# Gated linear attention followed by an MoE layer: two neighbouring tokens on one partition

## The chip, the cores and the metric

The kernel runs on one core of one Trainium2 chip. The metric is the device time of the core in microseconds (us), read from repeated executions. A span on a profile page is some 1.8 us shorter than the device time of the same execution, because the page counts from the first to the last instruction. PE is TensorE, DVE is VectorE, ACT is ScalarE, POOL is GpSimd, SP is SyncE (here it only issues DMAs).

## The reference

```python
# q, k, v, alpha: [B=4, H=8, S=768, D=48] float32, alpha in 0.8 .. 1.0
for t in range(S):                       # gated linear attention
    state = alpha[:, :, t, :, None] * state + k[:, :, t] (outer) v[:, :, t]
    y[:, :, t] = q[:, :, t] @ state
x = y.transpose(0, 2, 1, 3).reshape(3072, 384)
h = x @ w_in                             # 384 -> 2048
r = np.maximum(h, 0)
g = s * (r * r) + b
out = g @ w_out                          # 2048 -> 384, float32
```

The kernel cuts the sequence into 24 chunks of 128 tokens. Inside a chunk the running product of alpha, `b`, is the exponential of a running sum of logarithms. q is multiplied by `b` and k by `1/b`; then the causal part of a chunk is an ordinary masked matrix product, and one state per chunk carries the rest.

## The kernel before

A partition is a token of the chunk, so a load of one tensor and chunk moves 128 x 8 rows of 48 floats: packets of 192 bytes.

```python
def load(n, src, dst):                    # 4 tensors x 24 chunks, issued from SP
    nc.sync.dma_start(
        out=dst[n % NIN],                 # [128, H, D] fp32
        in_=src[b, :, c * C : (c + 1) * C, :].rearrange("h s d -> s h d"))

def st_ln(n):     # ACT: la = ln(alpha)
def st_cum(n):    # PE:  running sum, U_bf (upper triangular) @ la, and its last row
def st_exp_b(n):  # ACT: b_s  = exp(cum)
def st_exp_i(n):  # ACT: binv = exp(-cum), blast = exp(last row)
def st_vcast(n):  # POOL: vb = bf16(v)

def st_qb(n):     # DVE, both inputs in SBUF
    nc.vector.tensor_tensor(out=qk_sb[n % 3][:, 0, :, 0:D],
                            in0=q_in[n % NIN], in1=b_sb[n % 2], op=ALU.mult)
def st_kb(n):     # DVE, the same with k and binv
# ... st_T + st_Tcopy (PE, DVE) for the first 12 chunks, a DMA transpose from SP after that
# ... st_KV, st_t1, st_snew: the state (PE, DVE, POOL)
# ... st_A (PE), st_mask (DVE), st_y (PE), st_yevac (ACT), then a transpose of y

def relu(w):      # ACT: r = max(h, 0), bf16, 128x512          96 times
def square(w):    # DVE: gt = r * r, both inputs in SBUF       96 times
# mm1 (w_in) and mm2 (w_out) on PE are the bulk of PE's work
```

Nothing is ordered by hand. Each step is declared with an engine, an assumed duration in us and a priority. A list scheduler in the kernel then fixes one order for every engine before the program is built. The engines run those orders strictly, each its own.

```python
op("SP", 0.45, ranks[x, n], load, n, src, dst, w=[(x, n % NIN)], lat=1.2, dma=1.03)
op("ACT", 0.43, t - 1.0, st_ln, n, r=[("a", ii)], w=[("la", i2)])
op("DVE", 0.52, t + 0.2, st_qb, n, r=[("q", ii), ("b", i2)], w=[("qb", i3)])
op("SP", 0.5, -3000, st_Tdma, n, r=[("qb", i3), ("kb", i3)], w=[("qkT", i3)], lat=TLAT, dma=1.6)
op("DVE", 0.36, t + 1.0, square, w, r=[("r", w % 2)], ...)
op("SP", 0.5, -2000, ostore, x, r=[os], dma=0.55)
```

Loads, DMA transposes and stores all sit in SP's one order.

## Time and profile before

The median over 4 executions is 194.23 us (193.64 to 194.85).

| | before |
|---|---|
| median time | 194.23 us |
| PE / DVE / POOL busy | 173.8 / 133.0 / 54.7 us |
| time of all DMA packets on 16 engines | 155.4 us, of which 96.3 are the 192-byte input packets (15.7 ns each) |
| last w_out quarter in SBUF | 39.7 us |

First, lines of the profile page: the span, the busy times, and three of the rows that cut the span into 40 slices (a digit is the busy share in tenths; PEclk is the granted clock of PE).

```profile
span 192.8 us, 4631 instructions
...
PE 173.8 (90%) x1769; PEld 112.7 (58%) x1780; DVE 133.0 (69%) x232; ACT 114.0 (59%) x251; POOL 54.7 (28%) x90
...
DVE  4474636999979999999786735987565883354321
...
POOL 6332413406533465242434352313231100000000
PEclk9996999999999999999999999999999999999999
```

DVE stands at 9 in twelve slices, eleven of them between 33 and 92 us. Next, the busy time of each engine in four stretches (columns: stretch, length, PE, PE weight loads, DVE, ACT, POOL, granted clock, DMA share, GB/s).

```profile
0.00:40.00 40.00, 27.78 (x396) 21.75 (x397) 24.00 (x41) 19.39 (x40) 14.18 (x32) 0.96 0.98 212
40.00:90.00 50.00, 48.29 (x622) 36.66 (x621) 47.89 (x81) 39.58 (x96) 21.12 (x29) 1.00 0.99 202
90.00:150.00 60.00, 58.71 (x518) 33.15 (x525) 41.86 (x73) 38.87 (x88) 18.68 (x28) 1.00 0.97 194
150.00:192.00 42.00, 38.99 (x239) 21.10 (x239) 19.21 (x40) 16.13 (x29) 0.69 (x1) 1.00 0.20 61
```

So the DMA engines are close to full until 150 us (share 0.97 to 0.99), DVE is nearly full from 40 to 90 us, and PE is full after 90 us. The chain of waits (start, length, what) shows the DMA side of it; these are its longest DMA pieces:

```profile
29.75 9.89 DMA wst<-in_moe_w_out_dram
...
52.62 8.65 DMA a_in<-in_alpha_dram x2
...
98.82 4.58 DMA a_in<-in_alpha_dram
...
132.76 2.98 DMA a_in<-in_alpha_dram
```

Last, the groups of DVE instructions whose two inputs both lie in SBUF (busy us, mean ns of one, then the idle time ahead of them).

```profile
L579 DVE TENSOR_TENSOR gt<-r 128x512 bf16<-128x512 bf16 x96 | 43.9, 474 | 14.6 <-ACT r L567 13.8
...
L389 DVE TENSOR_TENSOR qk<-q_in,b_s 128x384 bf16<-128x384 f32 x24 | 16.0, 666 | 10.7 <-ACT b_s L379 6.1
L397 DVE TENSOR_TENSOR qk<-k_in,binv 128x384 bf16<-128x384 f32 x24 | 15.3, 641 | 6.3 <-DMA k_in<-in_k_dram 5.8
```

These means hide two populations. In the trace a q or k product lasts 554 or 552 ns on average when POOL is idle and 760 or 705 ns when it overlaps a POOL instruction; a square lasts 420 or 564 ns. (The count takes any POOL instruction but DMA issues, short semaphore instructions included; without those, a few of the 144 change sides.)

### The profile page before, as it was taken

What the parts mean: (1) busy time and instruction counts of PE and PEld (TensorE: products, weight loads), DVE (VectorE), ACT (ScalarE), POOL (GpSimd) and SP (SyncE); (2) the same over time, 40 slices, a digit from 0 to 9 for tenths busy, and PEclk for the clock granted to TensorE, in tenths of its full rate; (3) what the DMA queues carried; (4) which work ended last, traced back from release to release, by engine and by line L of the source; (5) the groups of instructions that cost most, each with busy time, mean ns of one, the idle gap of its engine ahead of it and who ended that gap; (6) DMA issues with size and microseconds to landing.
All of it is one profiled execution on the core that took longest, in us unless ns stands there. A gap on an engine that the chain in (4) does not pass through costs nothing.

```text
span 192.8 us, 4631 instructions
## 1 busy us (share of the span) xinstructions
PE 173.8 (90%) x1769; PEld 112.7 (58%) x1780; DVE 133.0 (69%) x232; ACT 114.0 (59%) x251; POOL 54.7 (28%) x90
## 2 busy tenths in 40 slices
PE   3857777899997999999999999999899999999992
PEld 3635666477685786775554564646564556445650
DVE  4474636999979999999786735987565883354321
ACT  2425525999675877797786756578346661576000
POOL 6332413406533465242434352313231100000000
PEclk9996999999999999999999999999999999999999
DMA  5999999989899999999999999997999612200212
GB/s 101 192 174 188 160 225 383 312 168 208 184 233 196 223 182 221 187 208 185 196 206 180 185 181 191 226 190 155 203 224 178 132 22 65 82 32 9 73 56 82
DMA packets 124151, 32.76 MB, mean 170 GB/s; under 512 B 117472, under 2 KB 124128, under 8 KB 124128
## 3 DMA queue, kind: packets, MB, share of 16 engines
q1 hardware_dynamic: 122240, 30.88, 74.5%
q0 software_dynamic: 1600, 1.57, 5.3%
q8 instruction: 14, 0.23, 0.5%
q14 instruction: 9, 0.07, 0.1%
q10 hardware_dynamic: 288, 0.00, 0.1%
HBM read 25.17 MB, written 4.72 MB: 155 GB/s over the span
## 4 chain that ended last, share of the span: by engine, by line
PE 53%; SPq 15%; DMA 14%; DVE 8%; ACT 5%; issue 4%; POOL 0%; DVEq 0%; ACTq 0%
PE bank L586 23%; PE bank L558 22%; SPq L294 12%; DMA a_in<-in_alpha_dram 8%; DMA wst<-in_moe_w_out_dram 5%; SPq L310 2%; PE a_ps L473 2%; DVE gt L579 2%; ACT r L567 1%; DVE am L482 1%; PE bank L506 1%; PE bank L365 1%; DVE qk L397 1%; DVE qkT L416 1%; DVE qk L389 1%
## 5 line engine op out<-in xcount | busy, mean ns | idle before, releaser
L567 ACT ACTIVATE r<-bank 128x512 bf16<-128x512 f32 x96 | 56.2, 607 | 35.0 <-PE bank L558 20.7
L558 PE MATMUL bank<-xd,w_in_bf 128*128 128x128 bf16 (+2 forms) x469 | 71.8, 295 | 5.3 <-DMA w_in_bf<-in_moe_w_in_dram 4.7
L586 PE MATMUL bank<-w_out_bf,gt 128*128 128x384 bf16 x384 | 70.4, 326 | 0.6 <-ACT w_out_bf L318 0.4
L579 DVE TENSOR_TENSOR gt<-r 128x512 bf16<-128x512 bf16 x96 | 43.9, 474 | 14.6 <-ACT r L567 13.8
L558 PEld LDWEIGHTS <-w_in_bf 128*128 128x128 bf16 x480 | 37.9, 99 | 25.5 <-DMA w_in_bf<-in_moe_w_in_dram 5.3
L586 PEld LDWEIGHTS <-gt 128*128 128x128 bf16 x384 | 35.6, 97 | 23.8 <-issue 1.3
L482 DVE TENSOR_TENSOR am<-a_ps,mask 128x1024 bf16<-128x1024 f32 x24 | 29.3, 1219 | 3.0 <-PE a_ps L473 2.6
L386 POOL CAST vb<-v_in 128x384 bf16<-128x384 f32 x24 | 14.6, 611 | 52.1 <-DMA v_in<-in_v_dram 43.2
L462 POOL TENSOR_TENSOR s_st<-t,blast 64x192 bf16<-64x192 bf16 x32 | 20.0, 626 | 26.3 <-DVE t L455 15.6
L358 ACT ACTIVATE la<-a_in 128x384 bf16<-128x384 f32 x24 | 12.7, 529 | 18.5 <-DMA a_in<-in_alpha_dram 17.9
L389 DVE TENSOR_TENSOR qk<-q_in,b_s 128x384 bf16<-128x384 f32 x24 | 16.0, 666 | 10.7 <-ACT b_s L379 6.1
L397 DVE TENSOR_TENSOR qk<-k_in,binv 128x384 bf16<-128x384 f32 x24 | 15.3, 641 | 6.3 <-DMA k_in<-in_k_dram 5.8
L595 DVE SCALAR_TENSOR_TENSOR o_sb<-bank,s_col,bias_w 128x384 f32<-128x384 f32 x12 | 7.4, 617 | 14.3 <-PE bank L586 14.2
L618 POOL TENSOR_TENSOR o_sb<-o_sb,bias_w 128x384 f32<-128x384 f32 x12 | 12.6, 1057 | 8.2 <-ACT o_sb L609 6.8
L379 ACT ACTIVATE b_s<-bank 128x384 f32<-128x384 f32 x24 | 11.9, 496 | 4.1 <-PE bank L370 3.6
L519 ACT ACTIVATE yn<-bank 128x384 bf16<-128x384 f32 x24 | 11.9, 495 | 2.5 <-PE bank L506 2.5
L382 ACT ACTIVATE binv<-bank 128x384 f32<-128x384 f32 x24 | 12.1, 503 | 0.1
L455 DVE TENSOR_TENSOR t<-bank,s_st 128x384 bf16<-128x384 f32 x16 | 8.8, 551 | 4.0 <-PE bank L432 2.7
L473 PE MATMUL a_ps<-qkT 64*128 64x128 bf16 x192 | 9.8, 223 | 0.9 <-DVE qkT L416 0.7
L416 DVE COPY qkT<-bank 128x1024 bf16<-128x1024 bf16 x12 | 8.2, 682 | 2.6 <-PE bank L409 2.6
L740 PE MATMUL bank<-zeros_bf 128*64 128x64 bf16 x112 | 6.8, 225 | 3.4 <-DVE zeros_bf L263 3.1
L365 PE MATMUL bank<-la,U_bf 128*128 128x384 bf16 x24 | 8.2, 340 | 1.5 <-ACT la L358 1.5
(47 smaller groups left out, 135.6 us busy)
## 6 DMA issues: line engine op xcount, KB each, us to landing
k_in<-in_k_dram SPq DMA_DIRECT2D x24, 192.0 KB, 4.2
a_in<-in_alpha_dram SPq DMA_DIRECT2D x24, 192.0 KB, 3.9
q_in<-in_q_dram SPq DMA_DIRECT2D x24, 192.0 KB, 4.0
v_in<-in_v_dram SPq DMA_DIRECT2D x24, 192.0 KB, 3.8
out_dram<-o_sb SPq DMA_DIRECT2D x24, 192.0 KB, 2.5
wst<-in_moe_w_out_dram SPq DMA_DIRECT2D x4, 768.0 KB, 11.2
w_in_bf<-in_moe_w_in_dram POOLq DMA_DIRECT2D x4, 384.0 KB, 6.8
qkT<-qk SPq DMA_TRANSPOSE x12, 4.0
```

The lines of the kernel that those rows point to most:

```text
L294: nc.sync.dma_start(out=dst[n % NIN], in_=src[b, :, c * C : (c + 1) * C, :].rearrange("h s d -> s h d"),)
L358: nc.scalar.activation(out=la_sb[n % 2][:, :, 0:D], in_=a_in[n % NIN], func=AF.Ln)
L386: nc.gpsimd.tensor_copy(out=vb_sb[n % 3], in_=v_in[n % NIN])
L389: nc.vector.tensor_tensor(out=qk_sb[n % 3][:, 0, :, 0:D], in0=q_in[n % NIN], in1=b_sb[n % 2], op=ALU.mult,)
L397: nc.vector.tensor_tensor(out=qk_sb[n % 3][:, 1, :, 0:D], in0=k_in[n % NIN], in1=binv_sb[n % 2], op=ALU.mult,)
L462: nc.gpsimd.tensor_tensor(out=s_sb[n % 2][rows, :, cols], in0=t1_sb[n % 2][rows, :, cols], in1=blast_sb[n % 2][rows].unsqueeze(2).to_broad ...
L473: nc.tensor.matmul(out=a_ps[:, e, p, :], lhsT=qkT[64 * e : 64 * e + 64, 1, p, :], rhs=qkT[64 * e : 64 * e + 64, 0, p, :], start=True, stop ...
L482: nc.vector.tensor_tensor(out=am_sb[n % 2].rearrange("a e p t -> a (e p) t"), in0=a_ps.rearrange("a e p t -> a (e p) t"), in1=mask.unsquee ...
L558: nc.tensor.matmul(out=hp[:, i * n : (i + 1) * n], lhsT=w_in_bf[:, kk, 128 * j : 128 * (j + 1)], rhs=xd_sb[g % 3][:, kk, 0:n], start=(kk = ...
L567: nc.scalar.activation(out=r_sb[w % 2], in_=bank("h", w), func=AF.Relu)
L579: nc.vector.tensor_tensor(out=dst, in0=r, in1=r, op=ALU.mult)
L586: nc.tensor.matmul(out=op[:, 0:d_model], lhsT=gt_sb[:, slot, j, :], rhs=w_out_bf[:, j, :], start=(j == 0), stop=(j == NJ - 1),)
```

## The change

The intent is larger packets and less work per token. A partition now holds two neighbouring tokens, so a packet is 2 x 48 floats, 384 bytes, and one load serves a pair of chunks. ln and the exponentials are taken once per pair of tokens; the token's own share of the decay is put back by products with alpha:

```diff
+    def load(m, src, dst):                 # pair m, 12 pairs
+            out=dst[m % NIN].rearrange("i h t d -> i h (t d)"),
+            in_=src[b, :, c * C : (c + 2) * C, :].rearrange("h (i t) d -> i h (t d)", t=2),

+    def st_ap(m, eng):                     # ap = alpha0 * alpha1
+        eng.tensor_tensor(out=ap_sb[m % 2], in0=a[:, :, 0], in1=a[:, :, 1], op=ALU.mult)
+    def st_pre(m, x, eng):                 # q0 *= alpha0, q1 *= ap, k0 *= alpha1
+        t, s, w = ((qt, 0, a[:, :, 0]), (qt, 1, ap_sb[m % 2]), (kt, 0, a[:, :, 1]))[x]
+        eng.tensor_tensor(out=t[:, :, s], in0=t[:, :, s], in1=w, op=ALU.mult)
+    # ap on POOL from pair 3 on, st_pre on POOL from pair 2 on (30 instructions)

+    def st_vcross(m):                      # v copied across the partition halves
+        eng.dma_start(out=vt_sb[m % 2][hi, 0], in_=vb_sb[m % 2][lo, 1])
+        eng.dma_start(out=vt_sb[m % 2][lo, 1], in_=vb_sb[m % 2][hi, 0])

+    def st_Tdma(m):                        # DMA transposes of 64 rows, two per pair
+        for c in range(2):
+            nc.sync.dma_start_transpose(
+                in_=qk_sb[m % 2][R * c : R * c + R].rearrange("a x u e d -> a (x u e d)"), ...)

     def ostore(x):                         # 48 stores of 64 rows instead of 24 of 128
+        for t in range(2):
+            nc.sync.dma_start(out=..., in_=out_sb[(x // 4) % NOUT][R * t : R * t + R])

-GROUPS = [1, 1, 2, 1, 1, 2, 4, 4, 4, 4]
+GROUPS = [2, 2, 2, 2, 4, 4, 4, 4]
-UNIT = 1.62
+UNIT = 1.4
-NIN = 9                                    # buffers of input chunks
+NIN = 4                                    # buffers of input pairs
-N_POOL_BIAS = 12
+N_POOL_BIAS = 4
# ... 8 common PSUM banks instead of 6 and a fixed pair, 64-row matmuls for the state,
# ... new durations and priorities for the list scheduler, which orders everything anew
```

## The prediction

> **What bounds the kernel now** (busy times in stretches, timeline, chain of waits).
>
> - 0 to 40 us, loading: DMA share 0.98. The first MoE matmul runs at 16.5 us, matmuls wait for w_in until 30.3, the last w_out arrives at 39.7.
> - 40 to 150 us: DMA share still 0.97 to 0.99; DVE 47.9 of 50 us until 90. The chain holds three long DMA waits for alpha (8.7, 4.6, 3.0 us).
> - 150 us to the end: DMA share 0.20, PE alone.
>
> PE is 90% busy on the page, but the Trainium skill ("Perfetto Trace Analysis", Identifying the Most-Contended Engine) warns that pipelined matmul busy time misleads. From start to start a 128x384 matmul costs 162 ns, not the page's 326; all useful matmuls sum to about 155 us. About 16 us of it is done by 40 us (24 lost), about 98 of 110 in the middle (12 lost); the tail is full.
>
> **What the change does.**
>
> DMA: 98304 input packets of 192 B become 49152 of 384 B. The packet records give 15.7 ns for 192 B and 65 to 75 ns for 1536 B; a line between them gives my estimate of 22 to 23 ns at 384 B. On 16 engines 96 us becomes 70: minus 26. The skill ("DMA: Bandwidth & Descriptors", Specifications) puts line rate at 512 B and more; 384 B stays below, so time does not halve. Given back: more DMA transposes (14 chunks instead of 12 for q/k, 12 instead of 10 for y; +4 us) and v copies across halves (+3). Total about 155 to 135 us.
>
> ACT: ln and exps once per pair: 12 x (0.53+0.50+0.50+0.20) = -21 us; 114 to about 92; not the limit.
>
> POOL: alpha product, pre-multiplies, v cast and v keep: 55 to about 90 us.
>
> DVE: +5 us (alpha product and pre-multiplies of the first pairs), +5 (8 more output evictions of 0.62), -2 (transposed copies). POOL contention, from overlaps in the trace: q/k products last 554 ns alone and 705 to 760 beside POOL, squares 420 against 564; more POOL work adds about 4 us. DVE: 133 to about 145 us.
>
> PE: same columns; 155 us stays.
>
> **Critical path.** Start: two pairs (8 x 1.45), w_in (10.2) and w_out (about 9) must arrive: last w_out near 34 us instead of 39.7. First MoE matmul stays near 17 us: a pair holds twice the data and has a longer chain. Gain 5 us. Middle: the waits for alpha disappear and some 7 of 12 lost us come back; the rest stays, since DVE needs about 6.3 us per chunk against PE's 6.45 until chunk 10. Tail unchanged. Of 26 us less DMA time only about 12 reach the span.
>
> **Prediction:** 182.5 us, 8 in 10 between 175 and 190. Faster by over 2%: 0.83; within 2%: 0.13; slower: 0.04.
>
> **What would show each step.** Input packets at 22 to 23 ns; last w_out at 33 to 36 us; waits for alpha in the middle gone from the chain, PE matmul lines over 60% of it; DVE over 140 us, and 95% busy between 40 and 90 us; qk and gt means above 670 and 475 ns; POOL 80 to 100 us.
>
> **What would make it wrong.** 384 B packets at 30 ns (no DMA gain): 190 or more. POOL pre-multiplies slower than 1 us each, with the alpha product on POOL ahead of ln: chunks come late, PE starves. DVE saturating: 187 or more. Longer latency per pair with only two buffers for q/k. On the good side, if DVE keeps up, PE's 155 us plus 15 us start and 4 us tail allows 174.

## The result, and the profile after

The median is 210.91 us over 4 executions (209.48 to 211.76). The ratio is 1.085, with a 95% interval of 1.078 to 1.092: slower by 8.5%. Ratios are the mean time of one kernel's fast runs over that of the other's fast runs of the same rounds on the same chip, so they are not quite the ratio of the medians that stand beside them.

| | before | predicted | after |
|---|---|---|---|
| median time, us | 194.23 | 182.5 | 210.91 |
| last w_out quarter in SBUF, us | 39.7 | 33 to 36 | 32.9 |
| input packets, ns each | 15.7 | 22 to 23 | 23.3 |
| all input packets on 16 engines, us | 96.3 | 70 | 71.7 |
| all packets on 16 engines, us | 155.4 | 135 | 154.9 |
| DVE busy, us | 133.0 | 145 | 165.5 |
| POOL busy, us | 54.7 | 90 | 100.7 |
| mean granted clock of PE | 0.990 | (not said) | 0.955 |

The same lines of the page:

```profile
span 209.1 us, 4551 instructions
...
PE 182.5 (87%) x1693; PEld 114.6 (55%) x1693; DVE 165.5 (79%) x271; ACT 99.3 (47%) x196; POOL 100.7 (48%) x142
...
DVE  4796698999999999999999999999967444444321
...
POOL 7661412694959999967695644656520000000000
PEclk9995799995899997999999999999999999999998
```

DVE stands at 9 in 24 slices instead of twelve, POOL is nearly full from 63 to 89 us, and the clock row has dips that before did not have. The stretches:

```profile
0.00:40.00 40.00, 31.23 (x377) 24.50 (x378) 31.11 (x57) 21.56 (x39) 18.34 (x46) 0.91 1.03 266
40.00:90.00 50.00, 41.48 (x442) 28.77 (x440) 49.31 (x68) 24.16 (x54) 43.34 (x49) 0.90 0.78 180
90.00:150.00 60.00, 55.30 (x533) 31.46 (x532) 58.83 (x94) 32.50 (x70) 36.95 (x45) 1.00 0.91 187
150.00:192.00 42.00, 41.58 (x271) 22.45 (x270) 22.26 (x48) 19.97 (x35) 2.10 (x4) 1.00 0.36 64
```

From 40 to 150 us DVE is busy 108.1 of 110 us. The others wait for it (ACT is idle for 29.8 us ahead of its relus until a square is done), while the DMA share falls to 0.78 between 40 and 90 us: the DMA engines are no longer the limit there. The same three groups, and one of the new POOL groups:

```profile
L652 DVE TENSOR_TENSOR gt<-r 128x512 bf16<-128x512 bf16 x96 | 56.8, 612 | 16.3 <-ACT r L640 15.8
...
L464 DVE TENSOR_TENSOR qk<-k_in,binv 128x384 bf16<-128x384 f32 x24 | 21.9, 942 | 0.1
L456 DVE TENSOR_TENSOR qk<-q_in,b_s 128x384 bf16<-128x384 f32 x24 | 20.0, 858 | 0.0
...
L402 POOL TENSOR_TENSOR k_in<-k_in,a_in 128x384 f32<-128x384 f32 x10 | 11.4, 1139 | 2.7 <-DMA k_in<-in_k_dram 2.5
```

The three DVE groups have the same counts and the same shapes as before, yet they take 98.7 us instead of 75.2: 23.5 us more for identical instructions. Ahead of the products DVE is idle for only 0.1 and 0.0 us in all, so it hardly ever waits for their inputs. Here the two engines stand side by side for a few microseconds (timeline of after: start, length, engine, line, operation):

```profile
70.01 2.40 DVE L456 TENSOR_TENSOR qk<-q_in,b_s 128x384 bf16<-128x384 f32 x2
70.68 1.31 POOL L695 TENSOR_TENSOR o_sb<-o_sb,bias_w 128x384 f32<-128x384 f32 x1
...
75.19 2.04 DVE L464 TENSOR_TENSOR qk<-k_in,binv 128x384 bf16<-128x384 f32 x2
...
75.50 1.31 POOL L402 TENSOR_TENSOR q_in<-q_in,a_in 128x384 f32<-128x384 f32 x1
```

Two products that would last about 1.1 us alone take 2.0 to 2.4 us while POOL works on SBUF tensors (an output bias, which before has too, in the first pair of lines; a new product in the second). Split as before, a q or k product lasts 548 or 550 ns alone and 939 or 1073 ns overlapping POOL; a square 419 or 782 ns. Alone they have not changed at all. And DVE's instructions with only one input in SBUF (the other in PSUM) do not lengthen: in after a mask of 128x512 lasts 679 ns beside POOL (31 of them) and 679 ns alone (17).

The chain of waits of after can only be followed back to 113 us; two of its pieces that have no like in before, and its longest wait for a DMA:

```profile
120.52 1.63 DVE qk L456 x2
122.15 1.76 DVE qk L464 x2
...
144.00 3.76 DMA k_in<-in_k_dram
```

One more view is needed, since PE's busy time misleads: on the page a 128x384 matmul lasts some 330 ns, but at full clock the next one starts 162 ns after it. From the trace I counted the useful PE work done by a given time: each matmul at that distance to the next one, or less where the next started sooner. This is an estimate worked out from the trace, good to about 2 us, since some records are missing and short matmuls are hard to price.

| useful PE work (us) done by | 40 us | 90 us | 100 us | 150 us |
|---|---|---|---|---|
| before | 15 | 60 | 68 | 113 |
| after | 18 | 50 | 57 | 100 |

After is 2 to 3 us ahead at 40 us, as meant. It is 11 us behind at 100 us and 13 behind at 150 us. The loss is made from 40 to 100 us, where DVE is full.

### The profile page after: what moved, and what is told of

It reads as the page before. It is cut to its first block, busy times and chain, and to the rows that moved or that the text cites. A ratio compares the mean times of both kernels' runs of the same rounds, so it can differ in the third digit from the quotient of the medians.

```text
span 209.1 us, 4551 instructions
## 1 busy us (share of the span) xinstructions
PE 182.5 (87%) x1693; PEld 114.6 (55%) x1693; DVE 165.5 (79%) x271; ACT 99.3 (47%) x196; POOL 100.7 (48%) x142
## 5 line engine op out<-in xcount | busy, mean ns | idle before, releaser
L640 ACT ACTIVATE r<-bank 128x512 bf16<-128x512 f32 x96 | 57.0, 599 | 56.6 <-DVE gt L652 29.8
L631 PE MATMUL bank<-xd,w_in_bf 128*128 128x256 bf16 (+1 forms) x384 | 76.8, 334 | 2.4 <-DVE gt L652 1.0
L652 DVE TENSOR_TENSOR gt<-r 128x512 bf16<-128x512 bf16 x96 | 56.8, 612 | 16.3 <-ACT r L640 15.8
L556 DVE TENSOR_TENSOR am<-bank,mask 128x512 bf16<-128x512 f32 x48 | 30.0, 679 | 1.1 <-PE bank L547 1.1
L464 DVE TENSOR_TENSOR qk<-k_in,binv 128x384 bf16<-128x384 f32 x24 | 21.9, 942 | 0.1
L402 POOL TENSOR_TENSOR q_in<-q_in,a_in 128x384 f32<-128x384 f32 x10 | 12.0, 1205 | 15.3 <-DMA q_in<-in_q_dram 15.1
L591 ACT ACTIVATE yn<-bank 128x384 bf16<-128x384 f32 x24 | 11.5, 488 | 14.4 <-PE bank L578 14.4
L447 POOL COPY vt<-vb 64x384 bf16<-64x384 bf16 x24 | 14.2, 591 | 6.2 <-ACT vb L440 4.9
L474 PE MATMUL bank<-ident_bf,qk 128*128 128x128 bf16 x80 | 9.0, 264 | 4.5 <-DVE qk L456 2.6
L402 POOL TENSOR_TENSOR k_in<-k_in,a_in 128x384 f32<-128x384 f32 x10 | 11.4, 1139 | 2.7 <-DMA k_in<-in_k_dram 2.5
L578 PE MATMUL bank<-vt,am 128*128 128x48 bf16 x192 | 9.7, 185 | 3.1 <-DMA vt<-vb 1.3
L402 POOL TENSOR_TENSOR q_in<-q_in,ap 128x384 f32<-128x384 f32 x10 | 11.4, 1144 | 1.9 <-DVE ap L394 1.7
L394 POOL TENSOR_TENSOR ap<-a_in 128x384 f32<-128x384 f32 x9 | 10.2, 1134 | 0.6
```

The lines of the kernel that those rows point to most:

```text
L402: eng.tensor_tensor(out=t[:, :, s], in0=t[:, :, s], in1=w, op=ALU.mult)
L447: nc.gpsimd.tensor_copy(out=vt_sb[m % 2][rows, e], in_=vb_sb[m % 2][rows, e])
L464: nc.vector.tensor_tensor(out=qk_sb[m % 2][:, 1].rearrange("a (p t) e d -> a t p e d", t=2)[:, t, :, :, 0:D], in0=k_in[m % NIN][:, :, t].r ...
L556: nc.vector.tensor_tensor(out=am_sb[(2 * m + c) % 3][:, e], in0=a_of(m, c, e), in1=mask.rearrange("a t j -> a (t j)").unsqueeze(1).to_broa ...
L591: nc.scalar.activation(out=yn_sb[m % 2][:, c], in_=y_of(m, c), func=AF.Copy)
L631: nc.tensor.matmul(out=hp[:, i * n : (i + 1) * n], lhsT=w_in_bf[:, kk, 128 * j : 128 * (j + 1)], rhs=xd_sb[g % 3][:, kk, 0:n], start=(kk = ...
```

## The experiments

The theories. A: POOL's new products read SBUF and hold up DVE's two-input instructions; DVE's longer durations are the loss. The rivals: B, POOL is simply late with its results, whatever it does to DVE; C, neither of these, but the longer chain per pair, the two buffers, the start and the clock; C1, the list scheduler's assumed durations are wrong and the new order is bad; C2, SP's single queue holds loads back behind transposes and stores; and D, attention runs too far ahead of the MoE work, or too little. All runs compared with before on the same chip. All passed the comparison with the reference; that says little about the kernels that are wrong (e1, e2 and their derivatives e6 and e16), because the comparison's tolerance lets such an error through.

### e1_tiny: after without the products on POOL

```diff
     def st_pre(m, x, eng):
+        if m >= N_DVE_PRE:
+            nc.gpsimd.memset(t[:, 0, s, 0:1], 0.5)     # one column, wrong on purpose
+            return
```

> The changed kernel with its 30 pre-multiplies on POOL (pairs 2 to 11) replaced by a write of one column, so the result is wrong on purpose and the order of all other instructions is the same. Theory A (POOL instructions that read SBUF hold up DVE's products and squares, and DVE is what the time follows): POOL falls from 101 to about 67 us, the means of the q/k products fall from 900 to under 750 ns and of the squares from 612 to under 520, DVE from 165 to about 147 us, time 211 to 190 to 197 us. Theory B (POOL's long serial work makes chunks late; contention is a by-product): similar time here. Theory C (neither: longer chain per pair, two buffers, starts and clock): time stays above 203 us.

Measured: 203.79 us, ratio 1.049 (1.041 to 1.057); one of the four runs was slow, and the median of the fast ones is 203.44. The order of all engines is unchanged. 7 us of the 16.7 come back. So theory A's range (190 to 197) is missed: the time stays above 203, where theory C had put it, and more than half of the loss is still there.

### e2_memset: POOL nearly as busy as in after, but without these reads of SBUF

```diff
+            nc.gpsimd.memset(pad_sb, 0.0)               # 128 x 768 fp32, in place of the product
             nc.gpsimd.memset(t[:, 0, s, 0:1], 0.5)
```

> As the run before, but each of the 30 pre-multiplies becomes a POOL fill of a scratch tile of about the same length (1.1 us) plus the one-column write: POOL stays as busy as in the changed kernel and as much in the chain, but reads no SBUF there. Theory A (the reads are what DVE waits for): DVE about 147 us and the time within 3 us of the run with one-column writes. Theory B (POOL's serial time delays the chunks): POOL about 100 us and time within 3 us of the changed kernel, 207 to 212.

Measured: 204.27 us, ratio 1.054 (1.046 to 1.062), although POOL is busy 89.2 us. (A fill lasted 0.74 us and not 1.1, so that is 11.5 us less than in after, but 22 us more than e1's 67.2.) The groups of e2:

```profile
L404 POOL MEMSET pad<- 128x768 f32 x30 | 22.2, 738 | 0.7
...
L657 DVE TENSOR_TENSOR gt<-r 128x512 bf16<-128x512 bf16 x96 | 46.8, 503 | 19.8 <-ACT r L645 19.5
...
L469 DVE TENSOR_TENSOR qk<-k_in,binv 128x384 bf16<-128x384 f32 x24 | 15.5, 673 | 3.5 <-DMA k_in<-in_k_dram 3.5
L461 DVE TENSOR_TENSOR qk<-q_in,b_s 128x384 bf16<-128x384 f32 x24 | 15.2, 659 | 2.0 <-POOL q_in L405 1.6
```

The products are back at 659 and 673 ns and the squares at 503, close to before, and DVE is busy 144.0 us: just what was predicted for after. The ten products that overlap nothing but fills last 548 ns, the fourteen alone 550; for squares it is 417 (12) and 420 (51). So it is the reading, not the time that POOL spends. e1 and e2 differ by 0.5 us for 22 us of POOL time: POOL's own lateness is worth next to nothing here. This agrees with the Trainium skill ("SBUF — State Buffer", Who interferes with whom): "A DVE instruction with two SBUF inputs contends with a GpSimd instruction that reads SBUF, not with one that only writes it". The price of the reads is 6 to 7 us of the time (210.91 to 204.27; 1.085 to 1.054). That leaves about 10 us unexplained, and by 100 us e2 has done 68 us of PE work, as much as before; the rest must be lost later. (What the reads cost once that later loss is gone is another matter: see e19.)

### e3_before_read and e4_before_memset: the same suspicion put into before

```diff
 # e3
     def st_vcast(n):
+        for i in range(2):
+            nc.gpsimd.tensor_tensor(out=vb_sb[n % 3], in0=v_in[n % NIN], in1=v_in[n % NIN], op=ALU.mult)
 # e4
+        for i in range(5):
+            nc.gpsimd.memset(vb_sb[n % 3], 0.0)
         nc.gpsimd.tensor_copy(out=vb_sb[n % 3], in_=v_in[n % NIN])
```

> The kernel before with two POOL products of 128x384 (two inputs from SBUF, about 1.1 us each, result overwritten by the cast that follows) ahead of each cast of v: +50 us of POOL work, nothing else changed, result right. Theory A: q/k products rise from 650 to over 800 ns, squares from 474 to over 560, DVE from 133 to over 150, time from 194 to 203 or more. Theory B and C: later v alone delays little (under 3 us), since v is needed late; DVE means stay.

> The kernel before with five POOL fills of the v tile (about 0.42 us each) ahead of each cast of v: again some +50 us of POOL time, but without reads of SBUF; result right. Theory A: DVE means stay near 650 and 474 ns and time within 3 us of 194. Theory B (POOL's time itself): as slow as the run with POOL products.

Measured: e3 206.40 us (1.066), e4 205.76 us (1.059). The squares in e3 and then in e4:

```profile
L581 DVE TENSOR_TENSOR gt<-r 128x512 bf16<-128x512 bf16 x96 | 51.2, 550 | 16.5 <-ACT r L569 15.9
```

```profile
L581 DVE TENSOR_TENSOR gt<-r 128x512 bf16<-128x512 bf16 x96 | 43.1, 464 | 20.5 <-ACT r L569 19.8
```

DVE's durations rise only with the reads (DVE 147.1 us in e3, 129.6 in e4, before 133.0), which repeats e2's finding. But the time rises by 11 to 13 us either way, so the time forecast for e4 (within 3 us of 194) was missed. In before, the added POOL work comes ahead of the cast of v, so it probably delays v and the state behind it, and that costs as much as slower products do; this was not tested. The pair shows the mechanism and not its price; the price is e2's.

### e5b_dur: the scheduler told the measured durations

The durations of POOL's, SP's and the squares' steps were set to measured ones (for example a product on POOL 0.77 to 1.15, a square 0.36 to 0.56, the transposes of a pair 2.5 to 4.0). A first try, with longer q/k products too (e5_dur), and the same idea on e7 (e8_logs_dur) failed to build: no order could be worked out.

```diff
-    op("POOL", 0.77, t + OFF["pre"], st_pre, ...)
+    op("POOL", 1.15, t + OFF["pre"], st_pre, ...)
-    op("SP", 2.5, -3000, st_Tdma, ...)
+    op("SP", 4.0, -3000, st_Tdma, ...)
-    op("DVE", 0.36, t + 1.0, square, ...)
+    op("DVE", 0.56, t + 1.0, square, ...)
     # ... eight more of this kind
```

> The changed kernel with the same instructions in another order: the durations from which its static order is worked out are set to what the trace showed (pre-multiplies 1.15 instead of 0.77 us, alpha product 1.13 instead of 0.8, squares 0.56 instead of 0.36, the transpose issues 4.0 and 3.0 instead of 2.5 and 1.6, and so on; the q/k products stay at 0.52, as the order can't be worked out with longer ones). Theory C1 (the order was made for shorter POOL and queue times, so engines wait in program order): 211 falls to 199 to 206. If the order is not it: within 3 us of 211[...].

Measured: 210.79 us (1.098), no change against after. Wrong durations alone are not the cause, at least not in a way that right ones mend.

### e6_stores_act: e1 with its 48 stores issued from ACT

```diff
-            nc.sync.dma_start(      # ostore
+            nc.scalar.dma_start(
```

> The kernel with one-column writes in place of the pre-multiplies (204 us), with the 48 output stores issued from ACT instead of SP, all else in the same order. Theory C2 (what is left, 9 us above before, comes from SP: one queue issues loads, stores, v copies and transposes in order, 13 us per pair against PE's 13, so the last pairs' loads come late and PE stalls between 110 and 150 us): last load issued before 130 instead of 138 us, time 195 to 199. Otherwise within 2 us of 204, or slower if ACT now waits for the output evictions.

Measured: 201.00 us (1.035, 1.029 to 1.041): 2.4 to 2.8 us better than e1, between the two forecasts. The first sign that SP's queue holds something up, but stores are not the main thing in it.

### e7_logs: pairs and 384-byte packets kept, the products gone, results right

ln is taken of both tokens, the running sum is two accumulated matmuls, the exponentials are taken per token. All alpha products vanish, from DVE and POOL.

```diff
-    st_ap, st_pre
     def st_cum(m, x):
+        for t in range(2):
+            nc.tensor.matmul(out=cb[:, 0 : H * D], lhsT=U_bf[:, 0 if t > x else 1],
+                             rhs=la[:, t, :, 0:D], start=(t == 0), stop=(t == 1))
     # ... exp and exp(-) of each token on ACT
```

> The pairs kept, but no products at all: logarithms of both tokens' alphas (one ACT instruction of 768 elements), two accumulated PE matmuls per cumulative sum, exponents per token; right result. POOL falls from 101 to about 57 us, ACT rises from 99 to about 115. If contention and POOL's time were all of it: 190 to 196 us. By the runs so far (removing the pre-multiplies gave 7 us): 198 to 204 us.

Measured: 201.44 us (1.039). DVE 135.8, POOL 54.0 us, products 613 and 575 ns. This kernel, whose result is right, fits e1 and e2: without the products the time is 9 us less than after's, and still 7 us more than before's. (Its order was worked out anew, so the size is less sure than theirs.)

### e9_logs_act and e10_logs_act_pool: e7 with stores on ACT, and more output bias on POOL

e9 issues e7's stores from ACT and tells the scheduler so; e10 also sets `N_POOL_BIAS` from 4 to 12, which takes 8 evictions from DVE.

> The run without products (201.4 us) with the 48 output stores issued from ACT instead of SP, and worked out as such in the order. C2 (SP's single queue is what holds the last pairs' loads and transposes back between 100 and 150 us): 201 falls to 194 to 198 and the stalls between 100 and 150 us (some 17 us of 50) go below 10. If the queue is not it: within 2 us of 201.

> As the run before it, with the outputs of the first 12 chunks instead of 4 scaled on ACT and given their bias on POOL, as in the kernel before: 5 us less DVE work in the stage where DVE is 96% busy (40 to 90 us), 8.5 us more POOL reads. If DVE's own added work is a cause: 2 to 5 us less than without. If POOL contention eats it: within 1.5 us.

Measured: 202.16 (1.052) and 202.44 us (1.053). Neither helps. By its own forecast e9 speaks against the queue; it moved stores, not loads, and had a new order. e10 is the "contention eats it" case: DVE loses 8 evictions, 4.9 us, but its squares go from 477 to 517 ns and its products from 627 and 575 to 673 and 600, beside 8 more biases on POOL, which read SBUF. DVE's busy time is 135.8 us, against 134.2 in e9: all of it came back, in a kernel whose result is right. (The two also differ in order.)

### e11_logs_192: e7 with two loads of 192-byte packets

```diff
+        for t in range(2):
+            nc.sync.dma_start(out=dst[m % NIN][:, :, t],
+                in_=src[...].rearrange("h (i t) d -> t i h d", t=2)[t])
```

> The run without products with two loads per tensor and pair, one for each token, so packets of 192 B as before the change (and 48 more issues on SP). If the larger packets are worth time: 384 B packets took 23.3 ns, 192 B ones 15.7, so 25 us more on the DMA engines, DMA share near 1 until 150 us, time 3 to 8 us above 201.4. If DMA isn't what binds after 40 us: within 2 us of it, except for the start (last w_out about 4 us later).

Measured: 237.01 us (1.237). This would be the worth of larger packets, 35 us against a forecast of 3 to 8, but the order is e7's, made for one load of 1.45 us, and e15 below shows that a wrong assumption about loads alone can cost 23 us; SP also has twice as many loads to issue. The run can't separate these. Only the start is plain: the last w_out quarter lands at 38.1 us instead of 31.6. The worth of the larger packets stays open.

### e12_lead16, e13_logs_lead20, e14_logs_lead12: attention less far ahead

In after PE runs on for 41 us after the last attention matmul, with MoE matmuls alone; in before for 30 us. If attention ran less far ahead (theory D), more MoE work would fill the gaps. `LEAD` is 28 in before, after and e7.

```diff
-LEAD = 28.0
+LEAD = 16.0        # e12, on after;   20.0 in e13 and 12.0 in e14, both on e7
```

> The changed kernel with the attention's lead in the working out of the order lowered from 28 to 16 units: same instructions, but 150 units of MoE matmuls stand on PE before the last attention matmul instead of 129 (145 in the kernel before). Theory D (the changed order puts attention ahead of MoE work that PE could do while attention is late; after the last attention matmul PE has 41 us left against 30 before): the rest after the last attention matmul falls from 41 to 27 to 33 us, time from 211 to 200 to 206. If PE's order is not a cause: attention ends later by as much as the rest gets shorter, time within 3 us of 211.

> The run without products (201.4 us, 131 units before the last attention matmul, 39 us after it) with the lead at 20: 142 units before it. D expects the rest to fall to 32 to 34 us and the time to 194 to 198; otherwise within 2 us of 201.

> The run without products with the lead at 12: 157 units before the last attention matmul. D expects 190 to 197 us, unless attention now ends late for its own place in the order; otherwise within 2 us of 201.

Measured: e12 214.29 (1.104), e13 205.39 (1.058), e14 208.86 us (1.076). All are worse than their bases. In e12 PE runs on for only 27 us after the last attention matmul, as meant, but that matmul comes at 180 us instead of 164. Theory D falls.

### e15_before_order: before with a wrong assumption about its loads

```diff
-    op("SP", 0.45, ranks[x, n], load, ..., dma=1.03)
+    op("SP", 0.45, ranks[x, n], load, ..., dma=0.72)
```

> The kernel before, same instructions, with its order worked out as if a load of 192 KB took 0.72 us of the DMA engines (the changed kernel's figure per chunk) instead of 1.03: then 129 units of MoE matmuls stand before the last attention matmul, exactly as in the changed kernel, instead of 145. D expects the rest after the last attention matmul to grow from 30 to about 40 us and the time from 194 to 199 to 206. If the order is not a cause: within 2 us of 194.

Measured: 217.14 us (1.120). The program does exactly the same work as before, in another order, and loses 23 us. Before has a tuned order; a new structure with an untuned one can lose that much from order alone. This is a warning for every comparison here that changes the order. e1 to e4, e6, e16, e19 and e20 do not change it, and e11 and e18 keep that of e7.

### e16_loads_act: e1 with the loads of pairs 7 to 11 issued from ACT

What is late after 100 us? The timeline of e2 shows it around 110 us.

```profile
106.68 2.17 SPq L495 DMA_TRANSPOSE qkT<-qk  x1
...
108.89 0.63 SPq L327 DMA_DIRECT2D a_in<-in_alpha_dram  x1
...
114.43 0.99 POOL L395 TENSOR_TENSOR ap<-a_in 128x384 f32<-128x384 f32 x1 [4.06 <-DMA a_in<-in_alpha_dram]
...
115.46 0.52 ACT L398 ACTIVATE la<-ap 128x384 bf16<-128x384 f32 x1 [6.50 <-POOL ap L395]
...
116.03 0.48 PE L412 MATMUL bank<-la,U_bf 128*128 128x384 bf16 x2 [3.44 <-ACT la L398]
```

The square brackets hold the idle time ahead of the instruction and what ended it. A load of alpha is issued at 108.89 us, right behind a transpose, and is there 5.5 us later. POOL, ACT and PE wait for it in turn; 3.44 us of PE are lost in this one place. SP's issues fill 55.7 of the 60 us from 90 to 150 us in e2: 34.2 us are transposes, 8.0 stores, 4.9 v copies, and only 8.6 are loads (sums over the trace). Whether a load waits for its own buffer or for its place in the queue can't be read off, so the loads were taken out of the queue:

```diff
     def load(m, src, dst):
+        eng = nc.scalar if m >= 7 else nc.sync
-        nc.sync.dma_start(
+        eng.dma_start(
```

> The kernel with one-column writes (203.8 us, where PE has done as much by 100 us as in the kernel before, 68 us, but only 103 against 113 by 150 us), with the loads of pairs 7 to 11 issued from ACT instead of SP at the same place of the order. Theory C2' (in the late stage a load stands on SP behind transposes and stores that wait for compute, and this is what loses the 10 us between 100 and 150): PE work by 150 us rises from 103 to 108 or more, time 194 to 199. Otherwise within 2 us of 204.

Measured: 195.56 us, ratio 1.0075 (0.9992 to 1.0158). That is about 8 us less than e1 with the same order of everything else, the same bytes and the same data, and level with before. On ACT an issue takes 0.37 us, and the loads now go out in step with the chunks (timeline of e16):

```profile
102.44 0.37 ACTq L327 DMA_DIRECT2D a_in<-in_alpha_dram  x1
...
110.82 0.53 ACT L398 ACTIVATE la<-ap 128x384 bf16<-128x384 f32 x1
...
114.33 0.37 ACTq L327 DMA_DIRECT2D a_in<-in_alpha_dram  x1
```

ln at 110.82 follows a load issued 8.4 us earlier, and does not wait for POOL or a DMA at all. The loads are not faster in flight: the last three of alpha land 4.4 to 4.5 us after their issue from ACT, and 4.3 to 5.4 us after it from SP in e2. They are issued 4 to 8 us earlier. The stretch from 90 to 150 us, first in e2, then in e16:

```profile
90.00:150.00 60.00, 52.63 (x463) 29.21 (x461) 43.60 (x87) 29.85 (x62) 26.75 (x49) 0.97 0.84 168
```

```profile
90.00:150.00 60.00, 59.13 (x543) 33.39 (x546) 52.10 (x98) 35.01 (x71) 21.28 (x38) 1.00 0.87 174
```

PE goes from 52.63 to 59.13 us of 60 (e1, from which e16 differs by this one edit, has 52.90, in a slow run). So SP's queue is a second cause. Whether it acts by the loads that stand in it, or by the transposes and stores that move up once the loads are gone (SP's issues now fill 44.3 us of the 60), the run does not tell.

### e18_logs_loads_act, e19_after_loads_act, e20_before_loads_act: the same move elsewhere

The same diff on e7 (e18), on after itself (e19), and on before for chunks 14 to 23 (e20).

> The run without products (201.4 us) with the loads of pairs 7 to 11 issued from ACT. C2': 194 to 198 us, the first version of pairs that would come near the kernel before; otherwise within 2 us of 201.

> The changed kernel itself, products and all, with only the loads of pairs 7 to 11 issued from ACT instead of SP. If the two causes add up (contention 7 us, loads on SP's queue 8 us): 211 falls to 202 to 205. If DVE, held up by POOL, already hides the late loads: within 3 us of 211.

> The kernel before with the loads of chunks 14 to 23 issued from ACT. Its loads stand on SP behind fewer waits, but its chain has 15% of SP issue and three waits for alpha after 50 us: if the queue costs it too, 194.4 falls to 188 to 192 and this is the fastest version; if DMA (share 0.97 with 192 B packets) is its limit there, within 2 us of 194.

Measured: e18 197.42 us (1.015, 1.008 to 1.021), e19 212.29 (1.092, 1.088 to 1.096), e20 194.69 (1.0015, 0.998 to 1.005). On e7, whose result is right, the move gives 4 to 5 us. On after itself it gives nothing: DVE is still busy 105.7 of the 110 us from 40 to 150 us, its products still last 889 and 920 ns, and a load that comes earlier waits for DVE. In before the queue is no limit. No version beat before.

Read the other way, e19 and e16 price the products with the late loads off SP's queue: 212.29 against 195.56 us, so 16.7 us instead of the 7 of e1. How much of that is reads and how much POOL's time was not split with fills, as e2 did it with the loads on SP.

### What the experiments add up to

| | time, us | useful PE work by 40 / 100 / 150 us |
|---|---|---|
| before | 194.23 | 15 / 68 / 113 |
| after | 210.91 | 18 / 57 / 100 |
| e2, no SBUF reads by the products on POOL | 204.27 | 19 / 68 / 106 |
| e16, no such products, and late loads off SP's queue | 195.56 | 20 / 67 / 112 |

The rows tell where each cause acts. The reads cost 11 us of PE work by 100 us. Without them, the queue costs another 6 us by 150 us. The two act in series: the second shows only when the first is gone (e19 against e16), and it hides part of what the first costs. The longer chain per pair and its two buffers (theory C) are still there in e16, so whatever they cost, the gain of the larger packets about makes up for it. And the head start of 2 to 5 us at 40 us is gone by 100 us in each of these.

## Why the prediction was wrong

**"More POOL work adds about 4 us" to DVE: this is the step that failed first.** DVE was predicted at 145 us and came to 165.5. The mechanism was named rightly; its size was not. The products and squares, which are the same instructions as before, grew by 23.5 us (4.0 + 6.6 + 12.9) where 4 were forecast; the other terms of the sum (+8) came out near +9. I had both durations, alone and overlapping, from the trace, but took the overlap of before as fixed. POOL's new instructions are long (1.1 to 1.2 us on average), read two SBUF tensors and come back to back where DVE is full, so 37 of 48 products overlap instead of 27, 51 of 96 squares instead of 36, and each overlap costs more: 939 and 1073 ns where 760 and 705 had been. e2, e4 (no reads, no growth) and e3 show that the reads do it. The prediction listed "DVE saturating: 187 or more" among its risks; that is what came, at a higher price.

**"POOL 55 to about 90 us" was 100.7.** A product on POOL takes 1.14 to 1.21 us on average where the scheduler counts on 0.77. Part of it is DVE's doing: the five of POOL's 39 products that overlap none of DVE's products or squares take 1.00 us, the longest of the others 1.56. Telling the scheduler the measured durations (e5b) changes nothing.

**"The waits for alpha disappear" held for the wrong reason.** They are gone from the part of the chain that can be followed (a wait of 3.76 us for k is there instead, at 144 us), because DVE comes later than the loads of alpha. When DVE is relieved they return (6.5 us at 109 us in e2), because SP's one order puts a late load behind transposes, stores (four per pair now, two before) and v copies. The prediction counted these as DMA bytes and not as places in a queue. e16 prices it at about 8 us. Why before's queue does no harm (e20), though its issues fill 55.2 of the same 60 us, was not tested.

**"Total about 155 to 135 us" of DMA time: the packets were right, the total was not.** Input packets take 23.3 ns, and 24.6 us were saved. But the total stayed at 154.9. The 256-byte packets of transposes rose from 21.9 to 37.3 us, not by the 4 us that was said: there are 17% more of them, and each takes 31.5 ns on average instead of 21.7. In bursts that hold nothing but q/k transposes the mean is 31.0 against 22.0 ns, but the median is 18 ns in most of them, in both kernels: it is a slow part of the packets that grew. That the 64 rows do it is not shown, because after also issues its two transposes right behind one another; in e16, where some go alone, such bursts have 20.5 to 35.1 ns. Stores (and the other 1536-byte packets) rose from 23.9 to 28.9 us, and the v copies added 4.4. This is counted, not tested: no run says what it cost in time, and in after the DMA engines were not the limit (share 0.78 from 40 to 90 us).

**"Gain 5 us" at the start was about right, and did not reach the end.** The last w_out quarter lands 6.7 us earlier, but ACT, with other work ahead of it, casts it only from 35.4 us; the first MoE matmul comes at 20.9 us and not near 17; and PE is 2 to 5 us ahead at 40 us. But from 40 to 90 us DVE sets the pace even in e16 (47.5 of 50 us busy, as in before with 47.9), and e16 has done 57 us of PE work at 90 us against before's 60. DVE in e16 has 146.1 us of work against 133.0 (8 more evictions, the alpha products of the first pairs, squares at 503 instead of 474 ns). But of the 8 evictions only two come before 90 us, and the alpha products before 40; from 40 to 90 us DVE does 22 squares in e16 and 27 in before, and more masks and products instead, so the order may play a part. What eats the head start is not shown by a run. With both causes taken away the design is level with before (e16, 1.0075) or 1.5% slower (e18, the one with a right result), so "of 26 us about 12 reach the span" was wrong even without the two faults.

**The clock.** The mean granted clock is 0.955 instead of 0.990, and 0.90 from 40 to 90 us, where e2 has 1.00. The Trainium skill ("TensorE: Matmul & The Clock Gate", Part 1: The HAM clock gate) says that PE falls to half clock after an idle window of about 3.4 us. The half-clock stretches in after's trace are 3.41 or 6.83 us long, which agrees with the window's length. But the window need not be idle throughout: in the 3.41 us before the drops at 47.0 and 77.8 us PE was busy for 48 and 54%, and no gap was longer than 1.1 us. The drops follow PE's stalls while DVE was full and add to their price; e2's 6 to 7 us include that.

**What stays open.** How much of the last 1 to 3 us (e16, e18 against before) is order: e15 shows that order alone can move 23 us, the three runs with `LEAD` found no better one, and none was searched for. How the 16.7 us between e19 and e16 divide into reads and POOL's time. And what 384-byte packets are worth by themselves (e11 is confounded).

## What to carry to other kernels

Before moving elementwise work to POOL, count DVE's instructions with two SBUF inputs: POOL instructions that read SBUF beside them made them up to twice as long on average here (550 to 1073 ns), so work moved to POOL where DVE is full comes back to DVE in part. Price a DMA not only by its bytes but by its place in the in-order queue of the engine that issues it, and ask which later load stands behind it. And compare new structures with an old, tuned order only after asking what the order alone can do: undo one suspect at a time with the order held fixed.

## What the Trainium skill lacked or had wrong

- "SBUF — State Buffer", Who interferes with whom, has the rule (and the runs agree), but no durations for such a pair. Here a 128x384 product on DVE (fp32 in, bf16 out) went from 548 to 939 ns and from 550 to 1073 ns beside POOL, a 128x512 bf16 square from 419 to 782 ns; over the whole kernel these instructions took 23.5 us more, worth 6 to 7 us of time (e2).
- "DMA: Bandwidth & Descriptors", Issuing engines are not separate DMA queues, says that issuing from several engines only saves the time it takes to initiate a DMA, "which is usually small relative to the DMA itself". Here the place in the issuing engine's order mattered more: moving 20 late loads from SP to ACT saved about 8 us (203.79 to 195.56), though the loads of alpha took no less time in flight (4.4 us). SP's issues filled 55.7 of 60 us, with 1.2 to 2.6 us for one transpose; an issued load took about 0.6 us of SP and 0.37 us of ACT. That page does not treat an in-order issuer as a possible bottleneck. (Where DVE was the limit, and in before, the same move gave nothing.)
- The same page, Specifications, gives 512 B as the least transfer for line rate, but no measured times below it for this chip. Measured per packet: 15.7 ns for 192 B and 23.3 ns for 384 B, so 12.2 and 16.5 GB/s per DMA engine.
- The same page, DMA Transpose (X-bar), has no cost per packet: here 22.0 ns on average for a 256-byte packet of single 128-row transposes, and 31.0 ns for those of two 64-row transposes issued together (why is not shown).
